# A channel-attention kernel on one core: four row slots instead of three, 112 packed rows instead of 144, the test's sum on ScalarE, the last store ahead of the branch

## The chip, the cores and the metric

The kernel runs on one core of a Trainium2 chip. The metric is device time in microseconds (us); the profiled execution is one run of the same program, taken with the hardware profiler.

## The reference

The input `x` is a bf16 image of 384 x 384 pixels with 384 channels (113.25 MB). The kernel scales each channel by one number:

```
gap = mean(x over pixels);  gmp = max(x over pixels)
scale = sigmoid( relu(gap @ w1) @ w2 + relu(gmp @ w1) @ w2 )      # w1: 384 x 96, w2: 96 x 384
out = x * scale
```

The scale needs every pixel before the first output can be made, and `x` is far larger than the on-chip memory. So there are two passes over `x`: one that forms the sum and the maximum, and one that multiplies.

## The kernel before, in words

**Units.** The 147,456 pixels lie on 128 partitions, 1152 pixel rows each. One such "row" is 384 bf16 values on each of 128 partitions, 98,304 bytes in all. All loads and stores are cut in rows, and a block of n rows is contiguous per partition.

**What stays on chip.** The second pass does not read again what the first pass could keep. Of 1152 rows, before keeps 132 rows in three slots of 44 (`slots`, L156; `stay_b`, L102), 21 rows in `hole`, 24 in `spare`, 18 in PSUM (`kept_ps`, `kept_b`) and 18 x 8 = 144 rows in packed form. Packing takes 8 rows of a slot into 6 rows of room (`pack`, L254 to L267): ScalarE splits off the low bytes and the high bytes, TensorE folds the high ones together, ScalarE writes the codes. It is exact only if certain bits of the high byte have one value. `look` (L269, VectorE) and `look_sums` (L276, TensorE) therefore collect a sum of deviations, and L315 puts it into `flag`. If `flag` is not zero, a branch at the end (L467 to L472) computes the packed rows once more from `x`; with this input it is not taken. What is left, 802 rows, is read a second time, and so are the 11 rows of `acc`.

**First pass** (L286 to L323). The list `loads` is walked in order. Each entry is a DMA on SP's queue (L289), sums on TensorE (L230), a running maximum on VectorE (`larger`, L252) and, for the last 8 rows of a packed slot, a look and a pack. The maximum is kept in `store[:, 0:22]` (`wide`). Late in the pass, at entry `n_wide`, L303 folds it to its first 11 rows (`acc`); the other 11 rows become free. From there VectorE works in pieces of 11 rows. The scheduler chooses the order of instructions on each engine here. A load into a slot waits until all readers of the old rows are done. SP issues its loads in order, so one that waits holds those behind it.

**Between the passes** (L326 to L355). VectorE folds 11 rows of maxima to one, TensorE turns them, two small products and a sigmoid give `scale_bc`. The first multiplication waits for it.

**Second pass** (L434 to L460). The order is written by hand for SP, ScalarE and VectorE. `order` starts with the blocks that stayed in the slots. For each block `put` (L369) multiplies on VectorE and issues the store on ScalarE's queue (L378); `read_into` lets SP load the next block into the freed slot (L388), waiting for that slot's store; `unpack` (L391 to L413) rebuilds 8 packed rows, ScalarE first (L399), then seven VectorE instructions (L402, L405). `put_held` stores `hole` and `spare`. Last come the 18 rows of PSUM, multiplied by L457 to L459 and stored by L460.

**The end.** `in_order.close()` (L461) ends the hand-written order ahead of L464, which loads `flag` into registers, and the branch. In the built program ScalarE's queue has L460 behind the branch L467. SP leaves the branch only when all eight DMA semaphores have been met, and ScalarE goes on from there.

Of the kernel before, what the change touches and what calls it, by code (L numbers as in the profile page):

```python
# [16 lines left out]


SLOT = 44
NS = 3  # L20
RING_BYTES = 256
HOLE_ROWS = 21

# [2 lines left out]

PACKED = 8
GROUP = 4
N_PACK = 18
HIGH = 0x3800  # L30
HIGH_MASK = 0x7800
HIGH_BITS = 0x8700
PLANE_ROWS = PACKED // 2 + PACKED // GROUP
# [2 lines left out]

ACC_ROWS = 11
WIDE = 22
SPARE_ROWS = 24
OPEN_ROWS = 55  # L40
PLAIN_ROWS = (44, 44, 22)
PSUM_ROWS = 16
BANK_ROWS = 2
LATE_ROWS = 3

PSUM_PIECES = (4, 9)
RAMP = ((14, 30),)
HALVES = (22, 22)
PLAIN = ((22, 22), (19, 11, 14), (14, 8))
OPEN_PIECES = (12, 11, 10)  # L50
HELD_PIECES = ((21,), (13, 11))
STAYING = ((22, 22), (11, 11, 11, 11), (11, 11, 9, 7, 6))

FIRST_STORES = ((1, 2, 3, 4, 4, 6, 8, 8, 8), (8, 8, 9, 9, 10), (10, 12, 22))
FIRST_READS = ((8, 8, 10, 10),)
# [7 lines left out]
def kernel(  # L63
# [7 lines left out]
    nc = tc.nc  # L71
    P = nc.NUM_PARTITIONS
    B_, H, W, C = x.shape
# [3 lines left out]
    A = ACC_ROWS  # L77
# [39 lines left out]
    FLAG = CQ * QP  # L117
# [15 lines left out]
    nc.scalar.activation(out=scale_bc[0:1, 0:1], in_=pick[0:1, 0:1], func=ACT.Sigmoid)  # L133

    n_planes = N_PACK * PLANE_ROWS
    store = consts.tile([P, A + SPARE_ROWS + n_planes, C], BF16)
    acc = store[:, 0:A, :]
    wide = store[:, 0:WIDE, :]
    spare = store[:, A:A + SPARE_ROWS, :]

    def planes(k):

        at = A + SPARE_ROWS + n_planes - (k + 1) * PLANE_ROWS
# [6 lines left out]
    high = hole[:, 0:PACKED, :]  # L150
    sign = hole[:, PACKED:PACKED + PACKED // GROUP, :]
    odd = hole[:, PACKED + PACKED // GROUP:2 * PACKED + PACKED // GROUP, :]
    diag = hole[:, HOLE_ROWS - 3:HOLE_ROWS - 1, :].rearrange("p n c -> p (n c)").rearrange("p (k m) -> p k m", m=P)
# [25 lines left out]
    loads = [(open_b, 0, WIDE, store, 0, None)]  # L179
    j = 0  # L180
    for m in PSUM_PIECES:
        loads.append((psum_b, j, j + m, slots[NS - 1], j, None))
        j += m
    assert j == early
    for k, b in enumerate(packed_b):
        j = 0
        for m in RAMP[k] if k < len(RAMP) else HALVES:
            j += m
            loads.append((b, j - m, j, slots[k % NS], j - m, k if j == SLOT else None))
        assert j == SLOT and m >= PACKED  # L190
    s = N_PACK % NS
    for b, pieces in zip(plain_b, PLAIN):
        j = 0
        for m in pieces:
            loads.append((b, j, j + m, slots[s], j, None))
            j += m
        assert j == b[1]
        s = (s + 1) % NS
# [5 lines left out]
    n_wide = len(loads)  # L204
    loads.append((psum_b, early, early + LATE_ROWS + BANK_ROWS, slots[s], SLOT - LATE_ROWS - BANK_ROWS, None))
    order = []
    for k, pieces in enumerate(STAYING):
        if k == 1:
            for buf, b, parts in zip((hole, spare), (hole_b, spare_b), HELD_PIECES):
                j = 0  # L210
                for m in parts:
                    loads.append((b, j, j + m, buf, j, None))
                    j += m
                assert j == b[1]
        s = (s + 1) % NS
# [70 lines left out]
    for i, (block, lo, hi, buf, at, k) in enumerate(loads):  # L286
        m = hi - lo
        rows = buf[:, at:at + m, :]
        nc.sync.dma_start(out=rows, in_=part(xr, block, lo, hi))  # L289
        if i < n_loads - SUM_TAIL:  # L290
            sums(rows, m, done, TOT - tail_rows)
        else:
            tail_sums(rows, m, i == n_loads - 1)
        if looked is not None:
            look_sums(looked)
            looked = None
        done += m
        if i == n_loads - SUM_TAIL - 1:
            turn_sums()
        if i == 0:  # L300
            continue
        if i == n_wide:
            larger(acc, acc, wide[:, A:WIDE, :])  # L303
            width = A
        for j in range(0, m, width):
            e = min(width, m - j)
            larger(store[:, 0:e, :], store[:, 0:e, :], rows[:, j:j + e, :])
        if k is not None:
            look(k, rows[:, m - PACKED:m, :])
            pack(k, rows[:, m - PACKED:m, :])  # L310
            looked = k
            if k == N_PACK - 1:
                look_sums(k)
                looked = None
                nc.vector.tensor_reduce(out=flag.bitcast(F32), in_=odd_ps, axis=AX.X, op=ALU.max)  # L315
# [75 lines left out]
    def unpack(item):  # L391
        _, s, k = item
        if k is None:
            return
        low, code = planes(k)
        rows = slots[s][:, SLOT - PACKED:SLOT, :].bitcast(U16)
        bits = acc[:, 0:PACKED, :].bitcast(U16)
        more = acc[:, PACKED:PACKED + n_grp, :].bitcast(U16)
        nc.scalar.activation(out=rows, in_=low, func=ACT.Copy, bias=float(HIGH))  # L399

        def field(out, shift, op, mask):
            nc.vector.tensor_scalar(out=out, in0=code, scalar1=shift, scalar2=mask, op0=op, op1=ALU.bitwise_and)  # L402
# [12 lines left out]
    again = [(b, k) for k, b in enumerate(packed_b)] + [(b, None) for b in (*plain_b[:-1], open_b, plain_b[-1])]  # L415
    stores, reads = list(FIRST_STORES), list(FIRST_READS)

    def rows_read(b, k):
# [20 lines left out]
    while k < len(order):  # L439
        block, s, _ = order[k]  # L440
        n = block[1] - (A if block is open_b else 0)
        put(order[k], stores.pop(0) if stores else (n,), None if k else ACC_STORES_AT)
        k += 1
        if k == LEAD:
            for j in range(k):
                read_into(order[j][1])
        elif k > LEAD:
            read_into(s)
        if 1 < k and k - 2 + NS < len(order):
            unpack(order[k - 2 + NS])  # L450
        if k == last - 2:
            put_held()
    assert not again
# [4 lines left out]
    multiply(rows[:, early:early + LATE_ROWS, :], kept_ps[:, 0:LATE_ROWS, :])  # L458
    multiply(rows[:, early + LATE_ROWS:n, :], kept_b)  # L459
    nc.scalar.dma_start(out=part(orr, psum_b, 0, n), in_=rows)  # L460
    in_order.close()  # L461


    odd_one = nc.values_load(  # L464
# [1 line left out]
    )  # L466
    with tc.If(odd_one != 0):  # L467
        for k, b in enumerate(packed_b):
            rows = slots[k % NS][:, SLOT - PACKED:SLOT, :]
# [4 lines left out]
_INS = ['x', 'w1', 'w2']  # L474
_OUTS = [((1, 384, 384, 384), 'bfloat16')]
# [25 lines left out]
```

## Time and profile before

| | |
|---|---|
| median of 3 runs | 741.32 us (740.7 to 741.96) |
| profiled execution, its own time | 741.41 us |
| span of its trace | 739.6 us |
| HBM read / written | 193.31 MB / 113.25 MB |
| busy share of the span: VectorE, ScalarE, TensorE | 76%, 24%, 22% |
| DMA queue of SP (q1), of ScalarE (q10): share of 16 engines' span | 62.0%, 35.9% |
| first store issued / last load landed / last store issued | 282.4 / 708.6 / 732.86 us |

The page cuts the span in 40 slices of 18.5 us; a digit is the busy share in tenths. "DMA share" in the tables by stretch is the mean busy share of the core's 16 DMA engines; values a little over 1 come from counting a packet where it starts. A releaser is what ended an engine's wait.

### The profile page before, as it was taken

The numbers are of one execution on the slowest core, as the hardware profiler recorded it, in microseconds if no ns is written. First come the engines' busy times: TensorE is split into PE (matmuls) and PEld (weight loads), VectorE is DVE, ScalarE is ACT, GpSimd is POOL, SyncE is SP. The second block draws the span as 40 slices with busy tenths as digits, with TensorE's granted clock in tenths as the row PEclk, the third lists the DMA queues.
The fourth block names the chain that finished last, engine by engine and source line by source line (L and its number), as shares of the span: only waits on it lengthen the run. The fifth ranks groups of instructions, "written<-read, shape, count | busy, mean of one in ns | idle before, by whom it ended". The sixth has DMA issues, their size and how long they took to land.

```text
span 739.6 us, 3511 instructions
## 1 busy us (share of the span) xinstructions
PE 165.0 (22%) x1320; PEld 64.3 (9%) x1320; DVE 562.8 (76%) x277; ACT 179.5 (24%) x123; POOL 0.7 (0%) x6
## 2 busy tenths in 40 slices
PE   3576666676753550000000000000000000000000
PEld 0222222222211120000000000000000000000000
DVE  5899999999999998897766666666666665444850
ACT  1566776666700000111111111111111111000000
POOL 0000000000000000000000000000000000000000
PEclk9878898888865555555555555555555555555555
DMA  9999999999999958999999999999999999999996
GB/s 380 421 429 427 426 426 426 427 428 427 424 421 426 420 235 318 393 438 429 423 438 433 428 427 439 433 425 440 436 427 427 431 433 429 407 428 435 426 440 264
DMA packets 20113, 306.79 MB, mean 415 GB/s; under 512 B 2592, under 2 KB 3072, under 8 KB 6784
## 3 DMA queue, kind: packets, MB, share of 16 engines
q1 hardware_dynamic: 13760, 193.32, 62.0%
q10 hardware_dynamic: 6336, 113.25, 35.9%
q8 instruction: 10, 0.16, 0.1%
q14 instruction: 7, 0.06, 0.0%
HBM read 193.31 MB, written 113.25 MB: 414 GB/s over the span
## 4 chain that ended last, share of the span: by engine, by line
DMA 61%; DVE 27%; ACT 6%; issue 1%; PE 0%; SPq 0%; DVEq 0%; ACTq 0%
DMA x<-in_x_dram 34%; DMA out_dram<-x 28%; DVE x L360 14%; DVE store L252 11%; ACT x L399 2%; ACT held L257 2%; ACT store L259 2%; DVE x L405 1%; ACT held L258 1%; DVE store L360 0%; DVE kept_ps L318 0%; PE bank_a L280 0%; DVE store L402 0%; SPq L289 0%; DVEq L464 0%
## 5 line engine op out<-in xcount | busy, mean ns | idle before, releaser
L360 DVE TENSOR_TENSOR x<-x,scale_bc 128x16896 bf16<-128x16896 bf16 (+10 forms) x39 | 220.5, 5682 | 42.5 <-DMA x<-in_x_dram 41.3
L252 DVE TENSOR_TENSOR store<-store,x 128x8448 bf16<-128x8448 bf16 (+11 forms) x63 | 226.8, 3600 | 15.5 <-DMA x<-in_x_dram 14.3
L399 ACT ACTIVATE x<-store 128x3072 uint16<-128x3072 uint8 x18 | 49.7, 2762 | 282.0 <-DMA out_dram<-x 248.1
L230 PE MATMUL bank_a<-x,small 128*1 128x512 bf16 (+2 forms) x882 | 88.0, 440 | 74.8 <-DMA x<-in_x_dram 73.6
L405 DVE TENSOR_TENSOR x<-x,store 128x3072 uint16<-128x3072 uint16 x18 | 31.6, 1758 | 91.9 <-ACT x L399 91.9
L257 ACT CAST held<-x 128x3072 bf16<-128x3072 uint8 x18 | 49.5, 2752 | 70.8 <-DMA x<-in_x_dram 70.8
L263 PE MATMUL bank_b<-held 128*128 128x384 bf16 x108 | 46.3, 429 | 21.7 <-ACT held L257 21.7
L259 ACT COPY store<-x 128x3072 uint8<-128x3072 uint8 x18 | 49.2, 2736 | 0.0
L263 PE MATMUL kept_ps<-held 128*128 128x384 bf16 x108 | 45.9, 426 | 0.0
L230 PEld LDWEIGHTS <-small 128*1 128x1 bf16 x939 | 30.7, 92 | 152.3 <-issue 134.3
L263 PEld LDWEIGHTS <-held 128*128 128x128 bf16 x216 | 26.2, 122 | 51.0 <-issue 45.5
L280 PE MATMUL bank_a<-held,small 128*1 128x512 bf16 x108 | 27.5, 392 | 0.4 <-DVE held L271 0.4
L402 DVE TENSOR_SCALAR store<-store 128x768 uint16<-128x768 uint16 x90 | 25.7, 352 | 0.0
L271 DVE TENSOR_SCALAR held<-x 128x3072 uint16<-128x3072 uint16 x18 | 17.1, 952 | 0.0
L240 ACT COPY w_sb<-bank_a 65x128 f32<-65x128 f32 x2 | 0.5, 262 | 68.4 <-PE bank_a L230 67.9
L258 ACT ACTIVATE held<-x 128x768 bf16<-128x768 bf16 x18 | 15.1, 838 | 0.0
L405 DVE TENSOR_TENSOR store<-store 128x768 uint16<-128x768 uint16 x18 | 10.0, 558 | 0.6
L252 DVE TENSOR_TENSOR store<-store 128x4224 bf16<-128x4224 bf16 (+4 forms) x8 | 10.3, 1282 | 0.2
L267 ACT ACTIVATE store<-bank_b 128x384 uint16<-128x384 f32 x18 | 8.8, 486 | 2.3 <-PE bank_b L263 2.2
L267 ACT ACTIVATE store<-kept_ps 128x384 uint16<-128x384 f32 x18 | 8.7, 482 | 0.0
L280 PEld LDWEIGHTS <-small 128*1 128x1 bf16 x108 | 8.1, 84 | 5.4 <-issue 2.4
L360 DVE TENSOR_TENSOR store<-store,scale_bc 128x1920 bf16<-128x1920 bf16 (+2 forms) x3 | 7.4, 2483 | 0.0
(45 smaller groups left out, 41.3 us busy)
## 6 DMA issues: line engine op xcount, KB each, us to landing
out_dram<-x ACTq DMA_DIRECT2D x21, 4224.0 KB, 23.1
x<-in_x_dram SPq DMA_DIRECT2D x39, 2112.0 KB, 24.3
x<-in_x_dram SPq DMA_DIRECT2D x17, 3456.0 KB, 22.9
x<-in_x_dram SPq DMA_DIRECT2D x3, 4224.0 KB, 24.9
x<-in_x_dram SPq DMA_DIRECT2D x8, 1056.0 KB, 20.9
out_dram<-x ACTq DMA_DIRECT2D x2, 2112.0 KB, 18.9
x<-in_x_dram SPq DMA_DIRECT2D x3, 1344.0 KB, 23.6
out_dram<-x ACTq DMA_DIRECT2D x5, 768.0 KB, 4.6
```

What stands on the lines that cost most here:

```text
L230: nc.tensor.matmul(sum_ps[q * QP:q * QP + 1, 0:g * P], lhsT=ones_bf[:, 0:1], rhs=rows[:, k:k + g, q * P:(q + 1) * P], start=(done + k == 0 ...
L252: nc.vector.tensor_tensor(out=out, in0=a, in1=b, op=ALU.max)
L257: nc.scalar.copy(out=high, in_=halves[:, :, :, 1])
L258: nc.scalar.activation(out=sign, in_=rows[:, PACKED - n_grp:PACKED, :], func=ACT.Sign)
L259: nc.scalar.copy(out=low, in_=halves[:, :, :, 0])
L263: nc.tensor.matmul(pack_ps[g], lhsT=diag[:, w, :], rhs=src, start=(w == 0), stop=(w == len(WEIGHTS) - 1))
L267: nc.scalar.activation(out=code[:, g, :], in_=pack_ps[g], func=ACT.Copy, bias=-OFFSET)
L280: nc.tensor.matmul(odd_ps, lhsT=ones_bf[:, 0:1], rhs=flat[:, c * 512:(c + 1) * 512], start=(k == 0 and c == 0), stop=(k == N_PACK - 1 and ...
L360: nc.vector.tensor_tensor(out=dst, in0=src, in1=scale_bc.unsqueeze(1).to_broadcast([P, n, C]), op=ALU.mult)
L399: nc.scalar.activation(out=rows, in_=low, func=ACT.Copy, bias=float(HIGH))
L402: nc.vector.tensor_scalar(out=out, in0=code, scalar1=shift, scalar2=mask, op0=op, op1=ALU.bitwise_and)
L405: nc.vector.tensor_tensor(out=out, in0=a, in1=b, op=ALU.bitwise_or)
```

## The change

1. A fourth slot: 44 rows of `store` behind `acc`. Three slots (`STREAM`) still turn in the first pass; all four turn in the second. The first 11 rows of the new slot lie where the upper half of `wide` is.
2. 14 packed slots instead of 18; `spare` has 4 rows instead of 24. Kept: 176 + 21 + 4 + 18 + 112 = 331 rows instead of 339. Read a second time: 810 rows instead of 802, beside the 11 of `acc`.
3. The order of loads at the end of the first pass: the new slot's rows 11 to 43, then `hole` and `spare`, then the new slot's rows 0 to 10, then the other three staying blocks. In the built program SP issues the first 22 rows of a staying block ahead of the new slot's rows 0 to 10, and VectorE takes the latter first. The fold of `wide` comes when `hole` has been taken in, ahead of `spare`.
4. The first packed slot is loaded by one DMA of 44 rows (before: 14 and 30); other cuts change as the diff shows.
5. ScalarE forms the test's sum (L315 was a VectorE reduction).
6. In the second pass `unpack` of block k+1 is put behind block k-1 in both kernels; with four slots its target was stored one block earlier.
7. `in_order.close()` stands behind the branch; in the built program ScalarE's queue has the last store ahead of the load of `flag` and the branch.

```diff
-NS = 3
+NS = 4
+STREAM = 3
-N_PACK = 18
+N_PACK = 14
-SPARE_ROWS = 24
+SPARE_ROWS = 4
-PLAIN_ROWS = (44, 44, 22)
+PLAIN_ROWS = (44, 44, 44, 44, 44, 22, 20)
-RAMP = ((14, 30),)
+RAMP = ((44,),)
-PLAIN = ((22, 22), (19, 11, 14), (14, 8))
-OPEN_PIECES = (12, 11, 10)
-HELD_PIECES = ((21,), (13, 11))
+PLAIN = ((44,), (22, 22), (22, 22), (22, 22), (22, 22), (22,), (20,))
+OPEN_PIECES = (17, 16)
+HELD_PIECES = ((13, 8), (4,))
+LAST_SLOT = (17, 16)
...
-    store = consts.tile([P, A + SPARE_ROWS + n_planes, C], BF16)
+    store = consts.tile([P, A + SLOT + SPARE_ROWS + n_planes, C], BF16)
...
-    slots = [xpool.tile([P, SLOT, C], BF16, name=f"x{s}") for s in range(NS)]
+    slots = [xpool.tile([P, SLOT, C], BF16, name=f"x{s}") for s in range(STREAM)]
+    slots.append(store[:, A:A + SLOT, :])
...
+    order = [(stay_b[STREAM], STREAM, None)]
+    j = WIDE - A
+    for m in LAST_SLOT:
+        loads.append((stay_b[STREAM], j, j + m, slots[STREAM], j, None))
+        j += m
+    for buf, b, pieces in zip((hole, spare), (hole_b, spare_b), HELD_PIECES):
+        j = 0
+        for m in pieces:
+            loads.append((b, j, j + m, buf, j, None))
+            j += m
+        if buf is hole:
+            n_wide = len(loads)
+    loads.append((stay_b[STREAM], 0, WIDE - A, slots[STREAM], 0, None))
     for k, pieces in enumerate(STAYING):
-        if k == 1:
...
-                nc.vector.tensor_reduce(out=flag.bitcast(F32), in_=odd_ps, axis=AX.X, op=ALU.max)
+                nc.scalar.activation(out=scrap, in_=odd_ps, func=ACT.Copy, accum_out=flag.bitcast(F32))
...
-        if 1 < k and k - 2 + NS < len(order):
-            unpack(order[k - 2 + NS])
+        if k + 1 < len(order):
+            unpack(order[k + 1])
...
-    in_order.close()
     odd_one = nc.values_load(
...
     with tc.If(odd_one != 0):
...
+    in_order.close()
```

More of the change, by code (lines that the diff above doesn't have):

```diff
@@ L135 @@
     n_planes = N_PACK * PLANE_ROWS
-    store = consts.tile([P, A + SPARE_ROWS + n_planes, C], BF16)
+    store = consts.tile([P, A + SLOT + SPARE_ROWS + n_planes, C], BF16)
     acc = store[:, 0:A, :]
     wide = store[:, 0:WIDE, :]
-    spare = store[:, A:A + SPARE_ROWS, :]
+    spare_at = A + SLOT
+    spare = store[:, spare_at:spare_at + SPARE_ROWS, :]
     def planes(k):
-        at = A + SPARE_ROWS + n_planes - (k + 1) * PLANE_ROWS
+        at = spare_at + SPARE_ROWS + k * PLANE_ROWS
         low = store[:, at:at + PACKED // 2, :].bitcast(U8).rearrange("p n (t c) -> p (n t) c", t=2)
@@ L152 @@
     odd = hole[:, PACKED + PACKED // GROUP:2 * PACKED + PACKED // GROUP, :]
+    scrap = hole[FLAG:FLAG + 1, 0:2, :].rearrange("p n c -> p (n c)")[:, 0:512]
     diag = hole[:, HOLE_ROWS - 3:HOLE_ROWS - 1, :].rearrange("p n c -> p (n c)").rearrange("p (k m) -> p k m", m=P)
@@ L155 @@
         nc.scalar.mul(out=diag[:, k, :], in_=ident_bf, mul=v)
-    slots = [xpool.tile([P, SLOT, C], BF16, name=f"x{s}") for s in range(NS)]
+    slots = [xpool.tile([P, SLOT, C], BF16, name=f"x{s}") for s in range(STREAM)]
+    slots.append(store[:, A:A + SLOT, :])
+    assert len(slots) == NS
     bank_a = psum.tile([P, 512], F32)
@@ L181 @@
     for m in PSUM_PIECES:
-        loads.append((psum_b, j, j + m, slots[NS - 1], j, None))
+        loads.append((psum_b, j, j + m, slots[STREAM - 1], j, None))
         j += m
@@ L188 @@
             j += m
-            loads.append((b, j - m, j, slots[k % NS], j - m, k if j == SLOT else None))
+            loads.append((b, j - m, j, slots[k % STREAM], j - m, k if j == SLOT else None))
         assert j == SLOT and m >= PACKED
-    s = N_PACK % NS
+    s = N_PACK % STREAM
     for b, pieces in zip(plain_b, PLAIN):
@@ L197 @@
         assert j == b[1]
-        s = (s + 1) % NS
+        s = (s + 1) % STREAM
     j = WIDE
@@ L203 @@
     assert j == OPEN_ROWS
-    n_wide = len(loads)
     loads.append((psum_b, early, early + LATE_ROWS + BANK_ROWS, slots[s], SLOT - LATE_ROWS - BANK_ROWS, None))
-    order = []
-    for k, pieces in enumerate(STAYING):
-        if k == 1:
[L209 to L215, printed above, removed]
+    order = [(stay_b[STREAM], STREAM, None)]
[3 more added lines that the diff above has]
+        j += m
+    assert j == SLOT
+    for buf, b, pieces in zip((hole, spare), (hole_b, spare_b), HELD_PIECES):
[3 more added lines that the diff above has]
+            j += m
+        assert j == b[1]
+        if buf is hole:
+            n_wide = len(loads)
+    loads.append((stay_b[STREAM], 0, WIDE - A, slots[STREAM], 0, None))
+    for k, pieces in enumerate(STAYING):
+        s = (s + 1) % STREAM
         order.append((stay_b[k], s, None))
@@ L413, in unpack @@
         add(rows, rows, bits)
-    again = [(b, k) for k, b in enumerate(packed_b)] + [(b, None) for b in (*plain_b[:-1], open_b, plain_b[-1])]
+    again = [(b, k) for k, b in enumerate(packed_b)] + [(b, None) for b in (*plain_b[:5], open_b, *plain_b[5:])]
     stores, reads = list(FIRST_STORES), list(FIRST_READS)
@@ L468 @@
         for k, b in enumerate(packed_b):
-            rows = slots[k % NS][:, SLOT - PACKED:SLOT, :]
+            rows = slots[k % STREAM][:, SLOT - PACKED:SLOT, :]
             nc.sync.dma_start(out=rows, in_=part(xr, b, SLOT - PACKED, SLOT))
```

## The prediction, made before the changed kernel was run

> **What bounds the kernel now.** I read the page's slices first, then the same by longer stretches, and then the two places where the DMA engines are not full.
>
> ```profile
> DVE  5899999999999998897766666666666665444850
> DMA  9999999999999958999999999999999999999996
> ```
>
> ```profile
> 40.00:200.00 160.00, 105.48 (x850) 42.93 (x843) 156.70 (x48) 109.73 (x79) 0.00 (x0) 0.84 1.01 427
> 200.00:266.00 66.00, 32.93 (x250) 9.60 (x250) 63.66 (x29) 1.80 (x3) 0.00 (x0) 0.59 1.01 422
> 266.00:286.00 20.00, 7.22 (x75) 4.53 (x74) 17.71 (x19) 1.78 (x7) 0.00 (x0) 0.50 0.48 164
> ...
> 350.00:728.00 378.00, 0.00 (x0) 0.00 (x0) 242.48 (x131) 41.43 (x15) 0.00 (x0) 0.50 1.00 430
> 728.00:740.00 12.00, 0.00 (x0) 0.00 (x0) 0.00 (x0) 0.00 (x0) 0.00 (x0) 0.50 0.41 171
> ```
>
> The columns are the stretch and its length, busy us of PE, PEld, DVE, ACT and POOL, the granted clock, the DMA share and GB/s. Both passes are bound by the DMA engines: share 1.00 or 1.01 at 422 to 430 GB/s. Time is lost only in the turn between the passes (266 to 286) and at the end (728 to 740). So an edit can act in three ways: more or fewer bytes at 430 GB/s, a longer or shorter turn, another end. In the first pass VectorE is nearly as full as the DMAs (156.70 of 160 us), which matters below.
>
> **Second pass, bytes.** 810 rows are read again instead of 802. Eight rows are 8 x 98,304 = 786 KB, at 430 GB/s **+1.8 us**. Nothing hides it, as the engines are full there. For the same reason the fourth slot itself gains nothing: ScalarE's unpack (L399) waits 248.1 us in all for stores, and these waits will mostly go, but behind them stand transfers that already fill the engines. Four unpackings less (each 5 x 0.352 + 0.558 + 1.758 = 4.08 us of VectorE, 2.76 us of ScalarE) come off engines that idle a third or more of that pass: 0. The cover is large: VectorE has 242.48 busy us in 378. Four packings less on ScalarE and TensorE: 0, for both idle between pieces.
>
> **The end.**
>
> ```profile
> 728.00:729.00 1.00, 0.00 (x0) 0.00 (x0) 0.00 (x0) 0.00 (x0) 0.00 (x0) 0.50 0.40 169
> 729.00:730.00 1.00, 0.00 (x0) 0.00 (x0) 0.00 (x0) 0.00 (x0) 0.00 (x0) 0.50 0.16 68
> 730.00:731.00 1.00, 0.00 (x0) 0.00 (x0) 0.00 (x0) 0.00 (x0) 0.00 (x0) 0.50 0.04 17
> 731.00:732.00 1.00, 0.00 (x0) 0.00 (x0) 0.00 (x0) 0.00 (x0) 0.00 (x0) 0.50 0.08 34
> 732.00:733.00 1.00, 0.00 (x0) 0.00 (x0) 0.00 (x0) 0.00 (x0) 0.00 (x0) 0.50 0.00 0
> 733.00:734.00 1.00, 0.00 (x0) 0.00 (x0) 0.00 (x0) 0.00 (x0) 0.00 (x0) 0.50 0.53 221
> 734.00:735.00 1.00, 0.00 (x0) 0.00 (x0) 0.00 (x0) 0.00 (x0) 0.00 (x0) 0.50 1.06 442
> ...
> 737.00:738.00 1.00, 0.00 (x0) 0.00 (x0) 0.00 (x0) 0.00 (x0) 0.00 (x0) 0.50 0.53 221
> ```
>
> ```profile
> 716.55 0.55 DVE L360 TENSOR_TENSOR x<-bank_b,scale_bc 128x768 bf16<-128x768 bf16 x1
> 732.86 0.34 ACTq L460 DMA_DIRECT2D out_dram<-x  x1
> ```
>
> The last 18 rows are multiplied at 717.1, but their store is issued at 732.86, when every other transfer is done. It carries 1,769 KB, which at 442 GB/s is 4.0 us (733.5 to 737.5), and takes 5.5 us from issue to landing, so 1.5 us is fixed cost. Issued at 717 it queues behind the other stores on the same 16 engines. These do not end together: most are done soon after 728, one or two go on until 732. If these stragglers keep their lag, their sixteenth of the new store follows directly: 732.0 + 4.0 = 736.0 instead of 737.5, **-1.5 us**. If the lag vanished, 288 KB (169 + 68 + 17 + 34) and 1,769 KB would go at 442 GB/s from 728.0, 4.65 us, to 732.65: -4.85 us. The least is the 0.9 us from 732.0 to the issue. I take -1.5, since one straggler is seen at the turn too (1 us stretches from 268 on move 233, 124, 55 and 5 GB/s). The load of `flag` (0.88 us on VectorE) and the branch now come after the store, under its transfer: 0.
>
> **The turn.** VectorE sets it. Its last maximum ends at 276.48, and 5.5 us of folding, small products and sigmoid follow to the first multiplication at 281.98; these do not change. Before, VectorE was late by its own work since 201:
>
> ```profile
> 199.39 0.95 DVE L271 TENSOR_SCALAR held<-x 128x3072 uint16<-128x3072 uint16 x1
> 201.88 0.70 DVE L315 TENSOR_REDUCE small<-bank_a 1x1 f32<-1x512 f32 x1 [1.55 <-PE bank_a L280]
> 202.61 30.50 DVE L252 TENSOR_TENSOR store<-store,x 128x8448 bf16<-128x8448 bf16 x10
> ```
>
> The change takes this 1.55 + 0.70 us from VectorE, and four looks of 0.95 us. That would let it meet the last landing, were there not a new wait. The new slot's rows 0 to 10 are loaded into the upper half of `wide`, so SP must wait for the fold. Queued behind that load on SP are 22 + 88 rows of staying blocks; queued on VectorE behind their maximum is all that is left.
>
> When does the fold end? TensorE starts on a piece when it lands, so its rows are a clock of landings by rows loaded, and rows cost the same in both kernels:
>
> ```profile
> 240.65 2.51 PE L230 MATMUL bank_a<-x,small 128*1 128x512 bf16 x18 [2.54 <-DMA x<-in_x_dram]
> 245.44 2.41 PE L230 MATMUL bank_a<-held,small 128*1 128x512 bf16 x18 [2.28 <-DMA held<-in_x_dram]
> ```
>
> These are 1019 and 1040 rows (0.228 us a row); the chain has 695 rows at 164.54, where after loads its first unpacked 44 rows whole. VectorE is there in time: with one 44-row load the first slot can begin at 21.57 (where before's 30-row piece landed, the same 79 rows) and takes 2 x 4.56 + 0.95 = 10.1 us; 13 more take 9.93 us each, the step between looks before (37.76, 47.69): 160.8. So the larger first load costs 0.
>
> From 164.5, by steps of before's chain (22 rows 4.60, 11 rows 2.39, hence 0.185 + 0.2005 a row): 220 rows in ten steps, 46.0, to 210.5; 22 rows, 215.1; 20, 17 and 16 rows, 11.2, to 226.3; the five late rows with two copies, 0.75 + 0.55 + 1.2, to 228.8; 17 and 16 rows of the new slot, 7.0, to 235.8; 13 and 8 rows of `hole`, 2.8 + 1.8, to 240.4; the fold 2.4: **242.8**. The queue behind `hole` holds 4 + 22 rows and would run to 1031 rows, 240.65 + 12 x 0.228 = 243.4. The held load is issued at 242.9, has 1.5 us of fixed cost and 1.08 MB at 430 GB/s, 2.5: landed at 246.9. Without the wait it would have landed at 243.4 + 11 x 0.234 = 246.0. From there VectorE has eleven 11-row pieces, 26.3, and the last three pieces as before, 276.48 - 271.50 = 5.0: 278.2, against 276.48: **+1.7 us**. Bounds: landing at 246.0 gives +0.8; a fold 2 us later gives +3.7. The reads themselves end about 0.9 us later, before VectorE does, so they are covered.
>
> The Trainium skill ("DMA: Bandwidth & Descriptors", section "Anatomy of one DMA", written for GpSimd's path) puts the fixed cost of a DMA at about 2.0 us, most of it the receipt of the last write; the row above gives 1.5 us. With 2.0 the turn would be +2.2 us; the row decides.
>
> **Sum.** +1.8 + 1.7 - 1.5 = +2.0 on the profiled 741.41 (span 739.6 and 1.8 around it): 743.4. The median of the runs shown, 741.32, lies 0.1 lower, so I forecast **743.3 us**. A change under 0.2%, 1.5 us, cannot be told from none.
>
> **Rivals.**
> - *The drain evens out* (the other side). The mechanism is at the end: with one more transfer queued, the engines end together. Its price is -4.85 in place of -1.5: 741.32 + 1.8 + 1.7 - 4.85 = 740.0, and with a fold in time 739.1. It decides once the end gains more than 3.5 us. For it: from 729 on the share is 0.16 or less, so nearly all engines have room. Against: stragglers at both drains. Faster, 0.15.
> - *The fold is in time.* VectorE is an estimated 1 us quicker, the queue never runs dry and the turn costs +0.8: 742.4. For it: only some 0.9 us separate the cases. Against: VectorE must then wait nowhere after 164.5. Within 0.2%, 0.32.
> - *The fold is later still*, or the whole first load leaves VectorE late: each us shows in full, +3.7 gives 745.3. Slower, 0.13.
> - *The fourth slot frees bandwidth.* Were the engines idle behind ScalarE's waits, those could come back: each 1% of the 378 us would give 3.8 us, 739.5 with one. The share of 1.00 speaks against it; in the chances it shares the 0.15 of the faster case.
>
> The forecast has 0.40. Slower is 0.40 + 0.13 = 0.53, same 0.32, faster 0.15. The range runs from the best sum, +1.8 + 0.8 - 4.85 = -2.25 (739.1), to the worst, +1.8 + 3.7 - 0.9 = +4.6 (745.9).
>
> **What would show it.** Right: L460's successor is issued within 1 us of VectorE's last multiplication; no stretch at 0 GB/s near the end; SP's load of 11 rows into `store` issued near 243 with a dip of DMA share just after; VectorE waiting there for a DMA for some 3 us; first multiplication near 283.7; second pass at 430 GB/s. Wrong: a DMA share clearly below 1 between 310 and 720, a first multiplication before 282.5, or an end in which all 16 engines stop together.

## The result, and the profile after

The changed kernel takes 745.64 us (median of 20 runs, 740.47 to 749.8); the kernel before, on the same chip, 741.64 us (20 runs). The ratio is 1.0055, 95% interval 1.0032 to 1.0078: **slower by some 4.0 us** (2.4 to 5.8). The forecast was +2.0 us (743.3), with a range of 739.1 to 745.9: the sign was right, and the time lies near the upper end. The profiled execution is a long one, 748.39 us with a span of 746.6, so 2.75 us above the median; a second profile of the same kernel (below) has 746.23 and 744.3.

The slices of the page, as shown of before (VectorE, and the 16 DMA engines; tenths of the slice):

```profile
DVE  3899999979999798999766666666664343344841
DMA  9999999999998969999999999999999999999996
```

A new notch stands in the thirteenth slice (an 8, at 224 to 243 us), two slices ahead of the dip at the turn, which both kernels have (5 and 8 before, 6 and 9 now). Then the same by stretches, with the columns that the prediction explains:

```profile
200.00:266.00 66.00, 31.93 (x231) 9.36 (x226) 61.31 (x24) 0.00 (x0) 0.00 (x0) 0.53 0.96 401
...
350.00:728.00 378.00, 0.00 (x0) 0.00 (x0) 222.60 (x101) 30.39 (x11) 0.00 (x0) 0.50 1.00 427
728.00:740.00 12.00, 0.00 (x0) 0.00 (x0) 2.12 (x3) 0.00 (x0) 0.00 (x0) 0.50 0.88 375
740.00:746.00 6.00, 0.00 (x0) 0.00 (x0) 0.00 (x0) 0.00 (x0) 0.00 (x0) 0.50 0.16 67
```

The end of the first pass, 200 to 266, has a hole that it did not have (0.96 in place of 1.01). The second pass has the same share as before, 1.00, at 427 GB/s where before had 430 (the second profile has 432 from 350 to 690, so the difference is this execution's). At the end six microseconds go at 67 GB/s.

**The turn.** First VectorE's timeline before (start, us, line, operation, what ended the idle time before it): its last maximum ends at 276.48, where a fold of the 11 rows begins, and the first multiplication starts at 281.98.

```profile
276.48 2.74 DVE L252 TENSOR_TENSOR store<-store 128x1920 bf16<-128x1920 bf16 x4
...
281.98 1.50 DVE L360 TENSOR_TENSOR x<-x,scale_bc 128x384 bf16<-128x384 bf16 x3 [1.17 <-ACT scale_bc L355]
```

Then SP's and VectorE's timelines after, and the stretches around SP's issue:

```profile
242.11 0.33 SPq L302 DMA_DIRECT2D store<-in_x_dram  x1
```

```profile
164.33 61.67 DVE L265 TENSOR_TENSOR store<-store,x 128x8448 bf16<-128x8448 bf16 x14 [3.74 <-DMA x<-in_x_dram]
...
247.09 2.36 DVE L265 TENSOR_TENSOR store<-store 128x4224 bf16<-128x4224 bf16 x1 [4.01 <-DMA store<-in_x_dram]
...
278.39 2.74 DVE L265 TENSOR_TENSOR store<-store 128x1920 bf16<-128x1920 bf16 x4
...
283.89 11.96 DVE L373 TENSOR_TENSOR store<-store,scale_bc 128x384 bf16<-128x384 bf16 x11 [1.17 <-ACT scale_bc L368]
```

```profile
238.00:240.00 2.00, 0.00 (x0) 0.00 (x0) 1.97 (x2) 0.00 (x0) 0.00 (x0) 0.50 0.82 346
240.00:242.00 2.00, 0.00 (x0) 0.00 (x0) 2.00 (x1) 0.00 (x0) 0.00 (x0) 0.50 0.16 68
242.00:244.00 2.00, 0.00 (x0) 0.00 (x0) 1.04 (x2) 0.00 (x0) 0.00 (x0) 0.50 0.46 68
244.00:246.00 2.00, 0.00 (x0) 0.00 (x0) 0.00 (x0) 0.00 (x0) 0.00 (x0) 0.50 1.01 418
```

SP issues the held load at 242.11, when the fold is done. The DMA engines have run dry between 240 and 241, VectorE then waits 4.01 us, its last maximum ends at 278.36 and the first multiplication starts at 283.89, 1.91 us later than before (281.98).

**The end.** VectorE's last multiplications and ScalarE's issue of the last store, then single microseconds:

```profile
722.16 4.16 DVE L373 TENSOR_TENSOR x<-x,scale_bc 128x7680 bf16<-128x7680 bf16 x1 [10.39 <-SPq L479]
...
729.57 0.55 DVE L373 TENSOR_TENSOR x<-bank_b,scale_bc 128x768 bf16<-128x768 bf16 x1
```

```profile
730.15 0.34 ACTq L473 DMA_DIRECT2D out_dram<-x  x1
```

```profile
737.00:738.00 1.00, 0.00 (x0) 0.00 (x0) 0.00 (x0) 0.00 (x0) 0.00 (x0) 0.50 0.67 287
738.00:739.00 1.00, 0.00 (x0) 0.00 (x0) 0.00 (x0) 0.00 (x0) 0.00 (x0) 0.50 0.44 186
...
741.00:742.00 1.00, 0.00 (x0) 0.00 (x0) 0.00 (x0) 0.00 (x0) 0.00 (x0) 0.50 0.26 111
...
743.00:744.00 1.00, 0.00 (x0) 0.00 (x0) 0.00 (x0) 0.00 (x0) 0.00 (x0) 0.50 0.13 55
```

The store is issued 0.03 us after the last multiplication, and no microsecond ahead of the last landing (745.2) stands at 0 GB/s any more. But the share falls slowly, from 0.67 at 737 to 0.13 at 743: some of the 16 engines are done seven microseconds ahead of the others. The gap is gone and a longer tail has come in its place. The multiplication of the last block read had waited until 722.16: the releaser named is SP's queue, which stands at the branch, but what came then is the last of the sixteen landings of a read issued at 698.49.

### The profile page after: what moved, and what is told of

The parts are those of the page before. It is cut to its first block, busy times and chain, and to the rows that moved or that the text cites. A ratio compares the mean times of both kernels' runs of the same rounds, so it can differ in the third digit from the quotient of the medians.

```text
span 746.6 us, 3270 instructions
## 1 busy us (share of the span) xinstructions
PE 158.8 (21%) x1239; PEld 58.8 (8%) x1239; DVE 544.2 (73%) x241; ACT 141.0 (19%) x101; POOL 0.7 (0%) x6
## 5 line engine op out<-in xcount | busy, mean ns | idle before, releaser
L373 DVE TENSOR_TENSOR x<-x,scale_bc 128x16896 bf16<-128x16896 bf16 (+6 forms) x25 | 165.7, 6651 | 113.4 <-DMA x<-in_x_dram 103.0
L265 DVE TENSOR_TENSOR store<-store,x 128x8448 bf16<-128x8448 bf16 (+9 forms) x58 | 221.3, 3815 | 19.2 <-DMA x<-in_x_dram 17.8
L243 PE MATMUL bank_a<-x,small 128*1 128x512 bf16 (+3 forms) x855 | 89.9, 463 | 67.0 <-DMA x<-in_x_dram 65.0
L373 DVE TENSOR_TENSOR store<-store,scale_bc 128x16896 bf16<-128x16896 bf16 (+8 forms) x18 | 62.2, 3498 | 28.0 <-DMA store<-in_x_dram 26.8
L412 ACT ACTIVATE x<-store 128x3072 uint16<-128x3072 uint8 x10 | 27.6, 2763 | 145.9 <-DVE x L373 70.7
L276 PE MATMUL bank_b<-held 128*128 128x384 bf16 x84 | 31.1, 371 | 17.5 <-ACT held L270 17.5
L276 PE MATMUL kept_ps<-held 128*128 128x384 bf16 x84 | 31.1, 371 | 0.0
L418 DVE TENSOR_TENSOR x<-x,store 128x3072 uint16<-128x3072 uint16 x10 | 17.6, 1758 | 13.0 <-ACT x L412 13.0
L418 DVE TENSOR_TENSOR store<-store 128x768 uint16<-128x768 uint16 (+1 forms) x18 | 14.9, 825 | 6.1 <-ACT store L412 5.6
L265 DVE TENSOR_TENSOR store<-store 128x4224 bf16<-128x4224 bf16 (+6 forms) x9 | 15.2, 1690 | 4.3 <-DMA store<-in_x_dram 4.0
L271 ACT ACTIVATE held<-x 128x768 bf16<-128x768 bf16 x14 | 11.7, 838 | 0.0
```

Of the source, the lines that this page charges most:

```text
L243: nc.tensor.matmul(sum_ps[q * QP:q * QP + 1, 0:g * P], lhsT=ones_bf[:, 0:1], rhs=rows[:, k:k + g, q * P:(q + 1) * P], start=(done + k == 0 ...
L265: nc.vector.tensor_tensor(out=out, in0=a, in1=b, op=ALU.max)
L271: nc.scalar.activation(out=sign, in_=rows[:, PACKED - n_grp:PACKED, :], func=ACT.Sign)
L276: nc.tensor.matmul(pack_ps[g], lhsT=diag[:, w, :], rhs=src, start=(w == 0), stop=(w == len(WEIGHTS) - 1))
L373: nc.vector.tensor_tensor(out=dst, in0=src, in1=scale_bc.unsqueeze(1).to_broadcast([P, n, C]), op=ALU.mult)
```

## The experiments

All runs stand beside runs of the kernel before on the same chip; ratios are to it. Line numbers move by one or two between kernels. To compare the DMA engines, two figures were worked out from the trace's DMA records, which list for every DMA sixteen landings, one of each engine: the *lag*, by how much the last of the sixteen comes after their median, and the engines' mean *idle time*, at the turn (from 235 us to the first store) and from 700 us to the end. These figures of one kernel are from one execution. The records do not name the engine that moved a packet.

| kernel (slots in turn) | median us | ratio | idle at the turn / from 700 | largest lag, 330 to 700 us | spread at the last landing |
|---|---|---|---|---|---|
| before (3) | 741.64 | 1 | 9.9 / 4.9 | 7.3 | late store alone |
| after (4) | 745.64 | 1.0055 | 11.6 / 5.2 | 11.7 | 7.6 |
| 1 store early (3) | 740.0 | 0.9974 | 10.9 / 1.8 | 2.9 | 2.5 |
| 2 store late (4) | 751.45 | 1.0115 | 11.8 / 8.7 | 11.8 | late stores alone |
| 3 fold early (4) | 743.38 | 1.0025 | 8.8 / 4.2 | 5.5 | 5.7 |
| 4 112 rows (3) | 741.68 | 1.0012 | 8.9 / 2.6 | 6.6 | late stores alone |
| 5 sum on ScalarE (3) | 739.69 | 0.9976 | 8.3 / 2.9 | 3.2 | late store alone |
| 6 stores coupled (4) | 746.52 | 1.0085 | 12.0 / 6.5 | 11.5 | 5.9 |
| 7 112 rows, store early (3) | 739.53 | 0.9985 | 8.2 / 0.9 | 1.3 | 1.4 |
| 8 144 rows, store early, sum (3) | 735.57 | 0.9939 | 8.1 / 1.0 | 1.4 | 1.4 |
| 9 read fence (4 held as 3) | 744.19 | 1.0032 | 12.0 / 1.9 | 5.4 | 1.2 |
| 10 112 rows, store early, sum (3) | 738.31 | 0.9957 | 8.3 / 1.1 | 7.2 | 1.4 |
| 11 after again (4) | 744.70 | 1.0043 | 11.6 / 7.3 | 11.8 | 8.5 |
| 12 fold early, read fence (4 held as 3) | 741.02 | 1.0008 | 9.0 / 1.1 | 3.5 | 1.4 |

**1. The last store ahead of the branch, alone** (before, with one line moved).

```diff
-    in_order.close()
     odd_one = nc.values_load(
...
     with tc.If(odd_one != 0):
...
+    in_order.close()
```

> The kernel before with one part of the change alone: in_order.close() behind the branch, so that the last store is issued ahead of it. My theory: the store queues behind the stragglers, -1.5 us against before; the last store is issued near 717 instead of 732.9, and the engines still end 4 us apart. The rival, that the drain evens out: -4.9 us, all 16 engines ending within 1 us. A second rival, that the end is worth nothing: within 0.5 us. Turn and second pass unchanged: first multiplication near 282.

Measured: 740.0 us (12 runs), ratio 0.9974 (0.9949 to 0.9999). The end, in single microseconds:

```profile
732.00:733.00 1.00, 0.00 (x0) 0.00 (x0) 0.00 (x0) 0.00 (x0) 0.00 (x0) 0.50 1.03 442
733.00:734.00 1.00, 0.00 (x0) 0.00 (x0) 0.00 (x0) 0.00 (x0) 0.00 (x0) 0.50 0.39 166
734.00:735.00 1.00, 0.00 (x0) 0.00 (x0) 0.00 (x0) 0.00 (x0) 0.00 (x0) 0.50 0.10 41
```

1.9 us by the ratio (0.1 to 3.8), where 1.5 was the forecast's step, and not 4.85. With three slots the engines end within 2.5 us of each other.

**2. The changed kernel with the close of the hand order ahead of the branch again.**

```diff
+    in_order.close()
     odd_one = nc.values_load(
...
-    in_order.close()
```

> The changed kernel with that part undone: four slots, 112 packed rows, the sum on ScalarE, but the last store behind the branch. My theory: 1.5 us slower than the changed kernel, which is about 5.5 us over before; a stretch at 0 GB/s just ahead of the last store. If the engines end far apart in the changed kernel only because one more store is queued, the ends here lie 4 us apart as before and the time is no more than 1 us from the changed kernel; if four slots let the engines drift apart, the drain ahead of the last store takes 6 us or more here too.

Measured: 751.45 us (6 runs), ratio 1.0115 (1.0059 to 1.0171), where 1.5 us over the changed kernel was expected: 5.8 us over it by medians, 4.4 by the ratios, whose intervals overlap. It does not price one store, since ScalarE's queue shows four behind the branch:

```profile
700.76 0.34 ACTq L445 DMA_DIRECT2D out_dram<-held  x1
728.15 0.34 ACTq L445 DMA_DIRECT2D out_dram<-store  x1
728.58 0.39 ACTq L391 DMA_DIRECT2D out_dram<-store  x1
729.06 0.43 ACTq L391 DMA_DIRECT2D out_dram<-x  x1
729.59 1.16 ACTq L473 DMA_DIRECT2D out_dram<-x  x1
```

`spare`, the blocks of 22 and 20 rows and the PSUM rows all wait until 728, though `spare` was multiplied at 700.65. From 722 to 728 the engines moved 22 GB/s. So part 7 of the change moves four stores in this kernel, where it moved one in the kernel before: in the built program the load of `flag` was put ahead of all four.

**3. The fold ahead of the fourth slot's loads**, so that SP need not hold the load into the upper half of `wide`.

```diff
     order = [(stay_b[STREAM], STREAM, None)]
+    n_wide = len(loads)
...
-        if buf is hole:
-            n_wide = len(loads)
```

> The changed kernel with the fold of the maximum to 11 rows put ahead of the new slot's loads (n_wide set there), so that the load of the new slot's rows 0 to 10 waits for nothing that is late. My theory, that this wait made the turn longer: no dip of the DMA share near 242, the first multiplication near 281.0 instead of 283.9, and about 2.9 us less than the changed kernel, though four small pieces more cost VectorE 0.7 us. The rival, that VectorE's own work sets the turn: first multiplication later than 283.5 and no gain.

Measured: 743.38 us (12 runs), ratio 1.0025 (0.9995 to 1.0056). The stretch that was nearly empty, SP's issue and the first multiplication:

```profile
240.00:242.00 2.00, 0.52 (x6) 0.12 (x1) 1.93 (x3) 0.00 (x0) 0.00 (x0) 0.50 1.03 439
```

```profile
230.51 0.33 SPq L301 DMA_DIRECT2D store<-in_x_dram  x1
```

```profile
280.51 11.85 DVE L372 TENSOR_TENSOR store<-store,scale_bc 128x384 bf16<-128x384 bf16 x11 [1.17 <-ACT scale_bc L367]
```

The load goes out 11.6 us earlier, the hole is gone, and the first multiplication comes 3.4 us earlier than in the changed kernel, 1.5 us earlier than in the kernel before. By medians 2.3 us of the 3.4 remain; the intervals of the two ratios overlap, so the trace carries this point and not the times.

**4. 112 packed rows with three slots** (before, with the packed and plain blocks of the changed kernel, and 48 rows in `spare` so that it reads the same 810 rows).

```diff
-N_PACK = 18
+N_PACK = 14
-SPARE_ROWS = 24
+SPARE_ROWS = 48
-PLAIN_ROWS = (44, 44, 22)
+PLAIN_ROWS = (44, 44, 44, 44, 44, 22, 20)
...
```

> The kernel before with 112 packed rows and the freed room given to spare (48 rows), so three slots turn and the same 810 rows are read again as in the changed kernel; its sum stays on VectorE, its last store behind the branch. My theory: bytes +1.8 us; the turn about 3 us shorter, since VectorE has four looks less and no wait for the fold (first multiplication near 279); so about 1 us under before, with the engines ending some 4 us apart as before. If four slots as such cost nothing in the second pass, the stretch from the first store to the first idle engine is as long as in the changed kernel (448 to 450 us without the last store); if they let the engines drift apart, it is 2 to 3 us shorter here.

Measured: 741.68 us (12 runs), ratio 1.0012 (0.9991 to 1.0032), not the 1 us under before that was expected. VectorE's wait for the sum did not shrink with the packing, it grew:

```profile
164.02 0.70 DVE L315 TENSOR_REDUCE small<-bank_a 1x1 f32<-1x512 f32 x1 [3.79 <-PE bank_a L280]
```

It cost 1.55 us before, and the first multiplication came at 281.25 instead of about 279. As in 2, four stores were found behind the branch, issued from 713.43 on. So its end is not the end of the kernel before; 7 mends that.

**5. The sum on ScalarE, alone** (before, with this line and a place to write to).

```diff
+    scrap = hole[FLAG:FLAG + 1, 0:2, :].rearrange("p n c -> p (n c)")[:, 0:512]
...
-                nc.vector.tensor_reduce(out=flag.bitcast(F32), in_=odd_ps, axis=AX.X, op=ALU.max)
+                nc.scalar.activation(out=scrap, in_=odd_ps, func=ACT.Copy, accum_out=flag.bitcast(F32))
```

> The kernel before with one part alone: the test's sum by ScalarE instead of the VectorE reduction. The prediction gave this part no term of its own. From before's trace VectorE, late by its own work from there to the turn, stood 1.55 us for the sums and worked 0.70 us: if the lateness is carried to the end, the first multiplication comes 2.2 us earlier (near 279.8) and the time falls by 2.2 us. The rival, that the turn waits for the last landing anyway: first multiplication after 281, no gain over 0.7 us.

Measured: 739.69 us (12 runs), ratio 0.9976 (0.995 to 1.0002), so 1.8 us less by the ratio, not clear of none by the times alone. The first multiplication comes 1.53 us earlier, at 280.45:

```profile
274.95 2.74 DVE L253 TENSOR_TENSOR store<-store 128x1920 bf16<-128x1920 bf16 x4
...
280.45 1.49 DVE L361 TENSOR_TENSOR x<-x,scale_bc 128x384 bf16<-128x384 bf16 x3 [1.17 <-ACT scale_bc L356]
```

**6. The fourth slot kept, the stores coupled to the multiplications**: VectorE writes one element of a slot whose store must have landed before it goes on.

```diff
+    def touch(s):
+        if again:
+            nc.vector.memset(slots[s][0:1, 0:1, 0:1], 0.0)
...
-        if k == LEAD:
-            for j in range(k):
+        if k == LEAD + 1:
+            for j in range(LEAD):
+                touch(order[j][1])
                 read_into(order[j][1])
-        elif k > LEAD:
-            read_into(s)
+        elif k > LEAD + 1:
+            touch(order[k - 2][1])
+            read_into(order[k - 2][1])
```

> The changed kernel with a fence of one-element VectorE writes in the second pass: before block i+1 is multiplied, VectorE waits until the store of block i-1 has landed, as unpacking forces it to with three slots. Everything else is as in the changed kernel (a few writes of 60 ns more). Theory that four slots cost time in the second pass because the 16 engines can run further apart: the landings of one store are again at most some 8 us apart (13 in the changed kernel), and the time falls by 2 to 3 us. The rival, that the length of the second pass does not depend on the number of slots in turn and what is over the prediction is chance of single runs: within 1 us of the changed kernel. A cost of the fence itself would show as DMA share under 1 between 350 and 700.

Measured: 746.52 us (8 runs), ratio 1.0085 (1.0055 to 1.0114), with a lag that still reaches 11.5 us. The theory that the stores' freedom lets the engines drift falls: the reads go as deep as before, and the tail is there.

```profile
736.00:737.00 1.00, 0.00 (x0) 0.00 (x0) 0.00 (x0) 0.00 (x0) 0.00 (x0) 0.50 0.79 333
737.00:738.00 1.00, 0.00 (x0) 0.00 (x0) 0.00 (x0) 0.00 (x0) 0.00 (x0) 0.50 0.08 31
...
742.00:743.00 1.00, 0.00 (x0) 0.00 (x0) 0.00 (x0) 0.00 (x0) 0.00 (x0) 0.50 0.03 14
```

**7. Three slots, 112 rows, the store early** (4 with the moved line of 1).

```diff
-N_PACK = 18
+N_PACK = 14
...
-    in_order.close()
     odd_one = nc.values_load(
...
+    in_order.close()
```

> Three slots with 112 packed rows and 48 rows in spare, and the stores ahead of the branch: the changed kernel without its fourth slot and without the wait for the fold, the sum still on VectorE. In the kernel with three slots and 112 packed rows above, four stores and not one had come to stand behind the branch, so its end was no fair comparison. By the sum of the prediction: bytes +1.8, end -1.5 to -1.9, turn -0.7 as measured there, so 0.5 to 0.8 us under before. If four slots cost nothing as such, the stretch from the first store to the end is here as long as in the changed kernel; if they cost 3 us, it is 3 us shorter.

Measured: 739.53 us (12 runs), ratio 0.9985 (0.9962 to 1.0009). It reads the bytes of the changed kernel and takes 5.2 us less by the ratios (6.1 by medians).

**8. The kernel before with 1 and 5.**

```diff
...
-                nc.vector.tensor_reduce(out=flag.bitcast(F32), in_=odd_ps, axis=AX.X, op=ALU.max)
+                nc.scalar.activation(out=scrap, in_=odd_ps, func=ACT.Copy, accum_out=flag.bitcast(F32))
...
-    in_order.close()
     odd_one = nc.values_load(
...
+    in_order.close()
```

> The kernel before with the two parts that seem to gain: the last store ahead of the branch and the sum on ScalarE; three slots, 144 packed rows. The parts act at different places, so they add: -1.9 - 2.2 = -4.1 us, near 737.3. If the earlier turn only moves a wait to the last landing, -1.9 - 0.7 = -2.6.

Measured: 735.57 us (12 runs), ratio 0.9939 (0.9914 to 0.9964): **faster than both kernels**, by 4.5 us by the ratio. The two gains alone are 1.9 and 1.8 us by their ratios, 3.7 together, and 4.5 came: within the intervals they add up. Its engines end together:

```profile
728.00:729.00 1.00, 0.00 (x0) 0.00 (x0) 0.00 (x0) 0.00 (x0) 0.00 (x0) 0.50 1.03 442
729.00:730.00 1.00, 0.00 (x0) 0.00 (x0) 0.00 (x0) 0.00 (x0) 0.00 (x0) 0.50 0.27 111
```

**9. The four slots held to the depth of three**: a read is issued only when the store of the block three ahead of it has landed.

```diff
-        if k == LEAD:
-            for j in range(k):
-                read_into(order[j][1])
-        elif k > LEAD:
-            read_into(s)
+        if k > LEAD and again:
+            touch(order[k - 2][1])
+            touch(order[k - 3][1])
+            read_into(order[k - 3][1])
```

> The changed kernel with its four slots held to the depth of three: from the third block on VectorE writes one element of the slot of the block before last and one of the slot before that, and only then is the next block's read issued, so a read starts when the store of the block three ahead of it has landed, as with three slots. Everything else, the turn with its late load too, is as in the changed kernel. If the depth of what is in flight is what lets the slowest engine fall 11 us behind in the second pass (with three slots up to 6) and costs some 3 us, the lag of the slowest engine stays at 6 us or less and the time is 741 to 743. The rival, that the four slots' cost lies elsewhere (the run's own slow packets, the turn) gives 745 to 746.5 with a lag that may still reach 11. If a read that starts so late lets the queues run dry, the DMA's share shows it and the time is over 747.

Measured: 744.19 us (12 runs), ratio 1.0032 (1.0013 to 1.005). Its last reads and its end:

```profile
690.00:720.00 30.00, 0.00 (x0) 0.00 (x0) 18.69 (x6) 0.00 (x0) 0.00 (x0) 0.50 0.97 402
```

```profile
738.00:739.00 1.00, 0.00 (x0) 0.00 (x0) 0.00 (x0) 0.00 (x0) 0.00 (x0) 0.50 1.03 442
739.00:740.00 1.00, 0.00 (x0) 0.00 (x0) 0.00 (x0) 0.00 (x0) 0.00 (x0) 0.50 0.11 42
```

The lag stays at 5.4 us and the engines stop within 1.2 us: the tail is gone, as the theory of depth has it. The time fell by 0.5 us only against the changed kernel beside it (11), so the forecast of 741 to 743 failed. The fence takes something too: from 690 to 720 the engines move 402 GB/s, against 427 in 11, which is (427 - 402) / 427 x 30 = 1.8 us.

The clean comparison is with 6. There, too, VectorE must wait for the store of the block before last, and the first multiplication comes at 284.17 (here 284.35); what 9 adds is that each read goes out one block later. The ratios are 1.0085 (1.0055 to 1.0114) and 1.0032 (1.0013 to 1.005), and their intervals do not meet: with this fence on VectorE, the deeper reads cost 3.9 us. The idle time from 700 us goes from 6.5 to 1.9 us. And the fence alone (6) stands 2.2 to 3.1 us over the changed kernel by the ratios, with intervals that overlap; that can be why 9 gains so little against 11.

**10. All of the change but the fourth slot and its loads** (7 with the line of 5).

```diff
-N_PACK = 18
+N_PACK = 14
...
-                nc.vector.tensor_reduce(out=flag.bitcast(F32), in_=odd_ps, axis=AX.X, op=ALU.max)
+                nc.scalar.activation(out=scrap, in_=odd_ps, func=ACT.Copy, accum_out=flag.bitcast(F32))
...
-    in_order.close()
...
+    in_order.close()
```

> The kernel before with 112 rows packed, the last store ahead of the branch and the sum on ScalarE, but three slots and its own order of the turn: all of the change but the fourth slot and the loads that go with it. Against the same with 144 rows packed (735.6 by its median, 0.9939 of the kernel before) it reads 8 rows more in the second pass: by the bytes' term of the prediction it takes 1.8 us more, 737 to 738 (ratio 0.995 to 0.997). If the 32 rows that no longer need unpacking give something back, it is 735.5 to 736.5. What the changed kernel takes over this one is the price of the fourth slot with its order of loads: by the theory that the slot costs 3 to 3.5 us and the turn's late load some 2 to 3 more, 745.6 less 737.5, about 8 us at most; by the theory that the slot itself costs nothing, 2 to 3 us.

Measured: 738.31 us (8 runs), ratio 0.9957 (0.9936 to 0.9979). Against 8 (0.9939) 8 rows more cost 0.0018 x 741.5 = 1.3 us by the ratios, 2.7 by the medians; the step said 1.8. Against the changed kernel, 1.0055 or 1.0043, **the fourth slot with its order of loads costs 6.4 to 7.3 us**.

**11. The changed kernel again**, with no edit, for a second profile.

> The changed kernel as it is, once more, on the same chip as the two others, for a second profile: its first profiled execution was 2.75 us longer than its median, and its engines ended 7.6 us apart. If that spread belongs to four slots, the slowest engine again falls 9 to 12 us behind the median one in the second pass, and the drain at the end is again over 5 us long; if it was that execution's own, the lag is 6 us or less and the time of this profile is 743 to 745. The median is expected at 744 to 747.

Measured: 744.70 us (10 runs), ratio 1.0043 (1.0014 to 1.0072). Its end, and its last reads:

```profile
734.00:735.00 1.00, 0.00 (x0) 0.00 (x0) 0.00 (x0) 0.00 (x0) 0.00 (x0) 0.50 0.49 209
735.00:736.00 1.00, 0.00 (x0) 0.00 (x0) 0.00 (x0) 0.00 (x0) 0.00 (x0) 0.50 0.11 45
...
738.00:739.00 1.00, 0.00 (x0) 0.00 (x0) 0.00 (x0) 0.00 (x0) 0.00 (x0) 0.50 0.07 28
...
742.00:743.00 1.00, 0.00 (x0) 0.00 (x0) 0.00 (x0) 0.00 (x0) 0.00 (x0) 0.50 0.03 14
```

```profile
690.00:720.00 30.00, 0.00 (x0) 0.00 (x0) 18.86 (x5) 0.00 (x0) 0.00 (x0) 0.50 0.99 427
```

A share of 0.06 to 0.07 is one engine in sixteen. In this trace one packet at a time is under way from 736 on, and the last of the sixteen landings comes 6.7 us after the fifteenth: one engine alone works off what it is behind with. The tail came in both executions of this kernel.

**12. Both repairs, 3 and 9.**

```diff
     order = [(stay_b[STREAM], STREAM, None)]
+    n_wide = len(loads)
...
+        if k > LEAD and again:
+            touch(order[k - 2][1])
+            touch(order[k - 3][1])
+            read_into(order[k - 3][1])
```

> The changed kernel with both repairs: the maxima of the 33 extra rows folded ahead of the fourth slot's loads, so that SyncE can issue those loads in time, and the four slots held to the depth of three. Accounts made of the engines' idle time say that the changed kernel loses some 3.3 us to the kernel with all of the change but the fourth slot (738.3 us) at the turn and 4 to 6 us at the end, where one engine is still draining alone; with both gone, and some 1 us of idle left by the held reads, it is 739 to 740.5 (ratio 0.997 to 0.999), its first multiplication at about 280.5 to 281 us, the lag of the slowest engine 6 us or less, and the share of the DMA goes from 1.0 to 0 within 2 us at the end. The rival: the drain at the end only shows a loss that sits elsewhere in the second pass, so that holding the depth gains nothing, as it gained 0.5 us (within its error) alone. Then it equals the one with the fold alone, 742.5 to 744.

Measured: 741.02 us (12 runs, 739.22 to 741.72), ratio 1.0008 (0.9986 to 1.003), first multiplication at 280.74, lag 3.5 us. The end:

```profile
733.00:734.00 1.00, 0.00 (x0) 0.00 (x0) 0.00 (x0) 0.00 (x0) 0.00 (x0) 0.50 0.97 415
734.00:735.00 1.00, 0.00 (x0) 0.00 (x0) 0.00 (x0) 0.00 (x0) 0.00 (x0) 0.50 0.20 83
```

It lies between the two expectations. The ratio fell from 1.0055 to 1.0008, with intervals that just do not meet (1.0032 and 1.003); from that of 11, 1.0043, they overlap. Against 3 they overlap too. And it stays 2.7 us over 10 by medians, 3.8 by the ratios, of which the fence's slower last reads (406 GB/s from 690 to 720; 417 in 10, 427 in 11, so 0.8 to 1.5 us) are a part.

## Why the prediction came out as it did

- **The bound: right.** The share is 1.00 from 350 to 728 in both kernels. The bytes' +1.8 us fits what 8 and 10 show, 1.3 us by the ratios and 2.7 by medians, but no run pins it closer. Time added up from the packets of single executions doesn't: after the first store's issue the engines are busy for 449.8 us in 7 and 452.6 in 10, which move the same bytes, and for 454.4 and 450.1 in the two executions of the changed kernel.
- **The turn: right in its sum (+1.7; measured +1.9), and in its mechanism.** The fold ended at 242.09 (242.8 was worked out), the issue came at 242.11 (242.9), the wait was 4.01 us, the last maximum ended at 278.36 (278.2). Sizes inside it were off and cancelled, which is luck. The held load was issued 0.8 us earlier than worked out and took 4.9 us from issue to its last landing (246.99) instead of 4.0: less 2.5 for its bytes, 2.4 of fixed cost, not 1.5. The rows came some 2 us earlier than the clock of landings had them, so the queue ran dry near 240, not at 243.4. And without the wait the turn would not have cost +0.8 but gained 1.5 us, as 3 shows: the sum on ScalarE is worth that much to VectorE (5), unless the held load covers it. So the wait's price is 3.4 us, where the text's two cases differ by 0.9. The rival with the fold in time, 742.4, met 743.4 in 3, with a gain at the turn that its end gave back.
- **The sum on ScalarE as no term of its own: right for this kernel, as the text gave the condition.** In a kernel without the held load it is a gain of 1.5 us at the turn and 1.8 by the ratio (5).
- **The end: the term that came out wrong.** "If these stragglers keep their lag, their sixteenth of the new store follows directly: [...] **-1.5 us**." On three slots this holds (1: 1.9 us). In the changed kernel the stragglers did not keep the lag of before. At the last landing the slowest engine was 6.3 and 7.8 us behind the median one, and the engines' idle time from 700 us on went from 4.9 us to 5.2 and 7.3, where it should have fallen by 1.5. That term was thus +0.3 to +2.4 instead of -1.5, off by 1.8 to 3.9 us. The sum, +2.0, missed the measured difference by 2.0 us (1.2 by the ratio in 11). That the time still lies within the range, which ends at 745.9, is in part luck: the range got there by a fold 2 us later, +3.7 at the turn, which did not come, and no case of it let the end cost time.
- **"The fourth slot itself gains nothing": right as to gains, but a loss was left out.** The text took a full share of 1.00 for proof that the depth of the queue is without effect. The share says that all 16 engines have work; it does not say that they are equally far: it was 1.00 in 11 where the lag was 11.8 us. The runs point to the depth of reads in flight: with the reads free, four slots gave a largest lag of 11.5 to 11.8 us in four of five executions (5.5 in the fifth, 3), three slots 1.3 to 7.3; with the fence on reads it was 5.4 and 3.5, while a fence on stores left it at 11.5. The last column of the table parts the kernels whose last store is early without overlap: 5.7 to 8.5 us where four slots read freely (after, 3, 6, 11), 1.2 to 2.5 with three slots or held reads (1, 7, 8, 9, 10, 12). These are single executions of each kernel. The times carry it in 9 against 6: 3.9 us for the depth of reads alone. The Trainium skill ("DMA: Bandwidth & Descriptors", section "Why a DMA increments its semaphore by 16 and not by 1") says that a DMA runs on up to 16 engines that finish independently, and is done when all have landed. The trace agrees and puts a number to it: landings of one store lay up to 13.5 us apart in 11.
- **The rival in which the drain evens out** is refuted by 1 for one more queued store. Its end does exist, in 7, 8 and 10, where the spread is 1.4 us; its price does not: there, too, the early store is worth 2.7 us (8 against 5, by the ratios), not 4.85.
- **Still open.** What makes one engine slower for a time is not known. By idle time the fourth slot's 6.4 to 7.3 us stand against 3.3 at the turn and 4.1 to 6.2 at the end, enough to hold all of it; by times the 3.4 us at the turn and the 3.9 of 9 against 6 would make 7.3. But taking both away (12) recovered 2.6 to 3.5 us by the ratios and left 3.8 against 10. The price of the fence (6), 2.2 to 3.1 us and not clear of none, would cover most of that; it was not measured in 12 itself. Whether a lighter way to limit the reads would win all of it was not tried.

## What to carry to other kernels

A further buffer bought nothing here, as the DMA engines were already full, and the depth of reads that it allowed cost time: the last transfer ends with the slowest of the DMA engines, and with deeper reads that one fell further behind. Look for a slow fall of the DMA share in the last microseconds, in steps of a sixteenth, before giving a late transfer a price. When a load reuses room that an engine must first clear, put the clearing ahead of all loads that could fill the queue meanwhile: here two lines in another place moved the first multiplication by 3.4 us.

## What was not expected of the hardware

- The sixteen landings of a single store came up to 13.5 us apart while the DMA share stood at 1.00. A lag lasts for 100 us and more: in the second profile of the changed kernel that of the stores was 9.8 us at 579, 11.8 at 600 and still 9.7 at 697. That of the reads between them was 3.5 to 4.7 us.
- The same program spreads over 740.3 to 749.8 us in 30 runs of the changed kernel, and over 736.8 to 744.4 in 31 of the kernel before; with both repairs (12) the range is 739.2 to 741.7 in 12 runs.
- A test's sum taken off VectorE, 0.70 us of work, was worth 1.5 us at the turn. The 1.55 us wait for TensorE's last product went with it, and VectorE then waited some 0.8 us for landings on the way (5).
